# Spreading a triangular solve, turning its first result on chip, and moving two copies in a recurrence

## The chip, the cores and the metric

The kernel runs on one core of one Trainium2 chip. The metric is device time in microseconds for one execution of the whole program, the median of several runs. TensorE (PE) multiplies, VectorE (DVE) and ScalarE (ACT) work on its results, GpSimd (POOL) does part of the elementwise work, and SyncE (SP) issues most of the DMA transfers. Each engine takes its instructions strictly in the order in which the program gives them; they wait for one another by semaphores.

## The reference

Three layers follow one another: a recurrence over 768 positions for 4 x 8 heads of width 40, a mixture of experts (8 experts, two per token), and a feed-forward layer. The change concerns the recurrence alone:

```python
for t in range(S):
    y[:, :, t] = np.einsum('bhd,bhde->bhe', rt, state)
    Sa = np.einsum('bhde,bhe->bhd', state, at)
    state_decay = state * wt[:, :, None, :] - np.einsum('bhd,bhe->bhde', Sa, bt)
    state = state_decay + np.einsum('bhd,bhe->bhde', vt, kt)
```

## The kernel before

The 768 positions are cut into 24 chunks of 32. Within a chunk the effect of `a` and `b` on later positions is a triangular system of 32 x 32 for each head; its inverse, T, turns the chunk's recurrence into plain products. The 32 heads are handled in two halves, so there are 48 **steps** `g`, two for each chunk. Four chunks make a **group** of eight steps, and one **solve** makes the T of all four chunks of a group at once.

Four strands of work are woven into one order per engine:

- `chain(g)` is a step itself. `s_mm` (L602) multiplies the state by the keys, and VectorE writes the new state, `ST` (L607), scaled by `WE`. `tr` (L619) transposes the state in two pieces; ScalarE copies each out as `TRs` (L621) and `KB` (L623). `u_mm` (L589) is the next step's product with Z; ScalarE copies it into `ST` (L592). `y_mm` (L559) makes the output of the step before, and `rv_mm` (L634) a mask product that VectorE writes as `RR` (L645). One PSUM pool, `cs`, of four buffers serves five such tiles in each step, so that `u_mm` gets the buffer that `RR` of the step before was read from.
- `prepare()` scales the chunks that come two groups later. `scale` (VectorE) makes the decay `E` with a scan (L227), `R` with a second one (L231), and then `abd` (L236) and `kb` (L240). ScalarE copies parts of `E` as `WE` (L242, L243) and `Ec` (L250). `prods` (L280) makes the triangular matrices, which ScalarE writes as `Ls` and SyncE stores as `lscr`. `turns` makes four turned pieces: two of `kb`, copied as `kn` (L314) and stored as `knd`, and two of `Ec`, copied as `EN` (L325).
- `solve_group(k)` computes T of group k while group k - 1 runs. `load_l` (L437, SyncE) loads the stored matrices as `Lu`. Then VectorE does seven pairs of product and reduction (L466, L468) and after them larger products and reductions (L478, L481), two of the products on GpSimd. The result, `Tt`, is stored as `tscr` (L517).
- `apply()` loads each chunk's T from `tscr` into the diagonal blocks of `Tbd` (`tbd`, L384, four DMAs) and multiplies by it (L406), which gives `Zt` (L408). `Tbd` has two buffers, for even and odd chunks.

What stands where is set by a position that each piece of the last three strands yields, in units of groups: between the parts of a step, `fill()` lets `pump` emit all pieces whose position has been reached. A solve's pieces are spread evenly between k - 1 + s[0] and k - 1 + s[1], with the load `ll` = .06 ahead; solve 1 has its own pair, `s_1`, and solve 0 runs before the first step. `tbd` of the first chunk of a group is placed by `tl`, and L406 by `zl`.

`own_tbd()` exists for solve 0 alone: a VectorE transpose (L374) of the first chunk's part of `Tt`, and four ScalarE copies (L378) that put it into `Tbd`.

Of the kernel before, what the change touches and what calls it, by code (L numbers as in the profile page):

```python
# [24 lines left out]
PR = 8  # L25
NC = S // C
NG = NP * NC
OPT = dict(yd=(), yv=33, gix=(1, 3, 4), ye=(2, 2),  lag2=1, plan=((0, 4, -0.881), (1, 5, -0.7929), (1, 6, -0.7905), (0, 5, -0.3416), (1, 7, -0.3331), (0, 6, -0.2825), (0, 7, -0.1981), (1, 8, -0.1391)), dl=0, dk=0, ns=(0, 0), nw=(1, 1), va=1, rb=0, ra=1, kb=0, ry=(2, 2), p1=(0, 0, 0, 1, 1, 1), lw=((4, 2, 2), (6, 6, 6)), fl=((0, 1, 2, 2, 2, 2, 2, 2), (0,) * 8), lag=6, ll=.06, hurry=40, pool=(1, 4), rvpool=False, f=(3, 3, 1, 1, 1, 0), s=(.05, .72), s_1=(-.12, .62), tl=1.9, zl=.96, zd=.32, t0=-.35, nd=3, z0=8.65)
NW = 2 * PR * (C + 1)
NTB = 2  # L30
GJ = 4
# [34 lines left out]
class Rec:  # L66
# [153 lines left out]
    def scale(self, i):  # L220

        nc = self.nc
        w, a, abd, kb = self.w33[self.wx(i)], self.a[self.wx(i)], self.abd[i % 2], self.kbt(i)[0:RW]
        E = self.p2.tile([128, PR, 2, C + 1], F32, name="E")
        R = self.p2.tile([128, NW + 2], F32, name="R")
        fl = E.rearrange("p a b c -> p (a b c)")
        nc.vector.tensor_tensor_scan(out=fl[0:RW], data0=w[:, 0:NW], data1=self.d1[0:RW].rearrange("p a b -> p (a b)"),  # L227
                                     initial=0.0, op0=ALU.mult, op1=ALU.add)
        d1b = self.d1b
        nc.vector.reciprocal(out=d1b[0:RW, C + 1::C + 1], in_=fl[0:RW, C::C + 1])  # L230
        nc.vector.tensor_tensor_scan(out=R[0:RW, NW::-1], data0=w[:, ::-1], data1=d1b[0:RW, ::-1],  # L231
                                     initial=0.0, op0=ALU.mult, op1=ALU.add)
        yield
        m = lambda t: t.rearrange("p a b s c -> p (a b) s c")
        Rv = R[0:RW, 2:NW + 2].rearrange("p (a c) -> p a c", c=C + 1)[:, :, None, 0:C]
        nc.vector.tensor_tensor(out=abd[0:RW], in0=a[0:RW], in1=E[0:RW, :, :, 0:C], op=ALU.mult)  # L236
        nxt = i + 4 if i < 2 else i + 2
        if max(GJ, i + 2) <= nxt < len(self.seq) and i not in (2, 3):
            self.load_w(nxt)
        nc.vector.tensor_tensor(out=m(kb), in0=m(kb), in1=Rv.to_broadcast([RW, 2 * PR, 2, C]), op=ALU.mult)  # L240
        we = self.pwe.tile([64, 2, PR, 2], F32, name="WE")
        nc.scalar.copy(out=we[0:D, :, :, 0].rearrange("p c a -> p a c"), in_=E[0:D, :, :, C])  # L242
        nc.scalar.copy(out=we[0:D, :, :, 1].rearrange("p c a -> p a c"), in_=E[64:64 + D, :, :, C])  # L243
        self.WE[i] = we
        self.scaled[i] = E

    def decays(self, i):

        Ec = self.Ecs[i % 2]
        self.nc.scalar.copy(out=Ec[0:RW].rearrange("p a (b c) -> p a b c", b=2), in_=self.scaled.pop(i)[0:RW, :, :, 0:C])  # L250
        self.Ec[i] = Ec
# [15 lines left out]
    def prods(self, i):  # L267
# [18 lines left out]
        for out, k in ((ls, 1), (am[:, :, 64:96], 0))[:1 if i < GJ else 2]:  # L286
            nc.scalar.mul(out=out, in_=pv[:, :, k], mul=-1.0)
        (nc.scalar if i < OPT['dl'] else nc.sync).dma_start(out=self.lscr[i // GJ][i % GJ * PR:i % GJ * PR + PR].rearrange("u q t i -> (q t) u i"), in_=ls)

# [12 lines left out]
    def turns(self, i):  # L302
# [12 lines left out]
        self.KN[i] = self.pkn.tile([128, HH * D], F32, name="knd")  # L315
        (nc.scalar if i < OPT['dk'] else nc.sync).dma_start(out=self.KN[i], in_=kn.rearrange("p h d -> p (h d)"))
        if i % 2 == 0:
# [28 lines left out]
    def prepare(self):  # L346
        n = len(self.seq)
        for first, i, at in OPT["plan"]:
            yield at
            for k, _ in enumerate((self.decayed if first else self.turned)(i)):  # L350
                yield at if first or at < OPT["t0"] else at + .03 * k
        for i in range(2 * GJ, n):
            pos = iter([i / GJ - 2 + s / (6 * GJ) for s in range(6)])
            nxt = self.decayed(i + 1) if i + 1 < n else iter(())
            yield next(pos)
            next(nxt, None)
            yield next(pos)
            turned = self.turned(i)
            next(turned)
            for _ in nxt:  # L360
                pass
            for _ in range(4):
                yield next(pos)
                next(turned, None)

    def solve(self):
        for k in range(len(self.seq) // GJ):
            yield from self.solve_group(k)

    def own_tbd(self):  # L370

        nc = self.nc
        tv = self.ptm.tile([128, C * C], F32, name="tm")
        nc.vector.transpose(out=tv[0:32].rearrange("p (t x) -> p t x", x=32),  # L374
                            in_=self.Tt[0:32, 0:C * C].rearrange("p (j t) -> p t j", t=C))
        for q in range(4):
            r = slice(32 * q, 32 * q + 32)
            nc.scalar.copy(out=self.Tbd[0][r, :, r], in_=tv[0:32].rearrange("p (t u q) -> p q u t", u=PR, q=4)[:, q])  # L378

    def tbd(self, i):  # L380

# [5 lines left out]
    def apply(self):  # L387

        nc = self.nc
        for i in range(len(self.seq)):  # L390
            at = 2 * i - OPT["zl"]
            if i and i % GJ == 0:
                yield self.tau(2 * i - OPT["tl"])
                self.tbd(i)
            self.wants[2] = lambda: 2 if self.solved <= i // GJ else self.ready <= i
            z = self.Z[(i + 2) % 3]
            am, T = self.AM[i % (2 * GJ)], self.Tbd[i % NTB]
            if i < GJ:
                yield self.tau(at) if i else self.early(OPT['z0'])
                self.halves(i, am, T)  # L400
                T = self.IG
            for sg in range(2):
                yield self.tau(at + sg * OPT["zd"]) if i else self.early(OPT['z0'])
                pt = self.pp.tile([128, 512], F32, name="pp")
                for p in range(4):
                    nc.tensor.matmul(pt[0:96, p * 128:p * 128 + 128], lhsT=am[:, sg * 4 + p],  # L406
                                     rhs=T[:, sg * 4 + p, :], start=True, stop=True)
                nc.scalar.copy(out=z[0:96, sg * 4:sg * 4 + 4].rearrange("p a x -> p (a x)"), in_=pt[0:96])  # L408
            self.ZT[i] = z
            if 0 < i % GJ < GJ - 1 or i and i % GJ == 0:  # L410
                self.tbd(i + 1)
# [28 lines left out]
    def solve_group(self, k):  # L440

        nc = self.nc
# [15 lines left out]
        q, h = C // 2, C // 4  # L458
# [25 lines left out]
        for b in range(2):  # L484
            o = b * q
            p = P[:, 4 * b:4 * b + 4].rearrange("p a (c x) -> p (a c) x", x=h)
# [16 lines left out]
        pool = OPT["pool"] if k else ()  # L503
# [12 lines left out]
        self.tscr[k] = self.pd.tile([GJ * PR, 4, C, C], F32, name="tscr")  # L516
        (nc.sync if k else nc.scalar).dma_start(out=self.tscr[k].rearrange("u q j t -> (u q) (j t)"), in_=self.Tt[:, 0:C * C])  # L517
        self.solved += 1
        if k == 0:
            self.own_tbd()  # L520
            self.tbd(1)


# [1241 lines left out]
```

## Time and profile before

| | us |
|---|---|
| median of 3 runs (1272.05 to 1279.73) | 1275.37 |
| profiled execution, its own time | 1278.76 |
| its span in the profile | 1277.0 |
| recurrence within the span, about | 55 to 460 |
| experts and feed-forward layer, about | 460 to 1277 |

| engine | busy us | share |
|---|---|---|
| PE | 1148.3 | 90% |
| DVE | 857.5 | 67% |
| ACT | 724.0 | 57% |
| POOL | 533.4 | 42% |

The shares are means over three layers of different kind. From about 500 us on TensorE is busy nearly all the time. In the recurrence all engines are busy for two thirds to five sixths of the time. What ends last there is read from the stretch itself: from the waits of each engine, and from the timeline at the places where a solve ends and the next begins. In the rows "x2" means two instructions of a kind in a row; the bracket at the end of a row is the time that the engine was idle before it, and who ended that.

### The profile page before, as it was taken

Reading aid. Unit: us, or ns where it says so; the run is one execution under the profiler, and the core shown is the slowest. Engines: PE = TensorE matmul, PEld = TensorE weight load, DVE = VectorE, ACT = ScalarE, POOL = GpSimd, SP = SyncE. Lnnn points to the kernel's source line nnn. Section 1 sums busy time; section 2 is a strip of 40 time slices with the busy share of each in tenths; the row PEclk is TensorE's granted clock in tenths of the full one; section 3 lists DMA queues with packets and bytes.
Section 4 is the critical chain, followed back from the end, with each engine's and each line's share of the span. In section 5 each row is a group of like instructions: output and inputs, shape, how many; then the busy total and the mean of one; then the engine's idle time right before and its main releaser. Section 6 shows DMA issues by size and latency. Waiting matters only on the chain. (4 is left out here: it accounts for less than half of the span.)

```text
span 1277.0 us, 34710 instructions
## 1 busy us (share of the span) xinstructions
PE 1148.3 (90%) x14222; PEld 1097.6 (86%) x14222; DVE 857.5 (67%) x1610; ACT 724.0 (57%) x1517; POOL 533.4 (42%) x518
## 2 busy tenths in 40 slices
PE   6578878887877978999999999989989999999998
PEld 5477767776867868999999999989889999999998
DVE  8769697878956527558778778684466665655543
ACT  6756767766765654424434434333566666666664
POOL 6325332322635145413345344443365555543331
PEclk9688999988989977999999999989999999999999
DMA  9775867665366583645366365662541111110000
GB/s 239 195 180 135 216 159 184 170 177 153 86 120 125 105 134 120 164 141 168 94 187 192 113 190 159 207 194 75 159 112 32 31 32 34 38 34 12 12 11 21
DMA packets 143904, 156.73 MB, mean 123 GB/s; under 512 B 69867, under 2 KB 112875, under 8 KB 143723
## 3 DMA queue, kind: packets, MB, share of 16 engines
q1 hardware_dynamic: 126362, 119.86, 36.7%
q0 software_dynamic: 10752, 22.32, 6.7%
q10 hardware_dynamic: 6608, 12.06, 3.2%
q8 instruction: 122, 2.00, 0.7%
q14 instruction: 60, 0.48, 0.1%
HBM read 111.07 MB, written 43.12 MB: 121 GB/s over the span
## 5 line engine op out<-in xcount | busy, mean ns | idle before, releaser
L1637 POOL TENSOR_TENSOR gl<-fh,gh 128x1024 fp32r<-128x1024 f32 x46 | 131.1, 2878 | 105.3 <-ACT gh L1653 102.0
L1292 PE MATMUL ph<-xh,w1h 128*128 128x256 f32 (+1 forms) x576 | 159.4, 290 | 2.5 <-issue 2.5
L1292 PE MATMUL ph<-xl,w1h 128*128 128x256 f32 (+1 forms) x576 | 159.1, 289 | 0.0
L1605 PE MATMUL fps<-fxh,ih 128*128 128x256 f32 x576 | 156.4, 286 | 1.8 <-DVE fh L1607 1.8
L1605 PE MATMUL fps<-fxl,ih 128*128 128x256 f32 x576 | 153.8, 281 | 0.5 <-DVE fxl L1148 0.3
L1636 DVE TENSOR_TENSOR fh<-fh,fp 128x1024 f32<-128x1024 f32 x48 | 95.0, 2014 | 60.5 <-ACT fp L1635 60.5
L1311 PE MATMUL py<-w2h,hh 128*128 128x320 f32 x400 | 131.2, 328 | 4.3 <-ACT hh L1144 3.5
L1311 PE MATMUL py<-w2h,hl 128*128 128x320 f32 x400 | 127.0, 318 | 1.6 <-DVE hl L1146 1.6
L1311 PE MATMUL py<-w2l,hh 128*128 128x320 f32 x400 | 126.7, 317 | 2.0 <-DVE w2l L1148 1.9
L1146 DVE SCALAR_TENSOR_TENSOR hl<-ph,hh 128x512 fp32r<-128x512 f32 (+1 forms) x104 | 69.2, 665 | 82.6 <-ACT hh L1144 82.3
L1607 DVE COPY fh<-fps 128x512 f32<-128x512 f32 x96 | 64.8, 689 | 79.5 <-ACT fp L1606 74.1
L1667 PE MATMUL fpy<-oh,gl 128*128 128x320 f32 x384 | 114.6, 310 | 0.0
L1667 PE MATMUL fpy<-oh,gh 128*128 128x320 f32 x384 | 114.3, 310 | 0.0
L1667 PE MATMUL fpy<-ol,gh 128*128 128x320 f32 x384 | 113.9, 308 | 0.0
L1292 PEld LDWEIGHTS ph<-xh,w1h 128*128 128x128 f32 x576 | 111.2, 193 | 2.8 <-issue 2.7
L1292 PEld LDWEIGHTS ph<-xl,w1h 128*128 128x128 f32 x576 | 111.2, 193 | 0.3 <-DVE xl L1148 0.3
L1292 PE MATMUL ph<-xh,w1l 128*128 128x256 f32 (+1 forms) x384 | 111.0, 289 | 0.0
L1605 PEld LDWEIGHTS fps<-fxh,ih 128*128 128x128 f32 x576 | 109.0, 189 | 2.1 <-DVE fh L1607 2.0
L1605 PEld LDWEIGHTS fps<-fxl,ih 128*128 128x128 f32 x576 | 109.0, 189 | 1.1 <-DVE fxl L1148 1.1
L1605 PE MATMUL fps<-fxh,il 128*128 128x256 f32 x384 | 107.8, 281 | 0.0
L1144 ACT ACTIVATE hh<-ph 128x512 fp32r<-128x512 f32 (+1 forms) x104 | 59.9, 580 | 81.1 <-PE ph L1292 78.2
L1606 ACT ACTIVATE fp<-fps 128x512 f32<-128x512 f32 x96 | 56.1, 597 | 79.1 <-PE fps L1605 73.5
(299 smaller groups left out, 3215.5 us busy)
## 6 DMA issues: line engine op xcount, KB each, us to landing
share<-in_w_dram SPq DMA_DIRECT2D x9, 1280.0 KB
share<-in_w_dram SPq DMA_DIRECT2D x9, 1024.0 KB
wa<-in_wa_dram SPq DMA_DIRECT2D x40, 195.2 KB
knd<-kn SPq DMA_DIRECT2D x24, 320.0 KB
kb<-in_kb_dram SPq DMA_DIRECT2D x40, 192.0 KB
KB<-knd SPq DMA_DIRECT2D x24, 320.0 KB
yb<-y SPq DMA_DIRECT2D x22, 320.0 KB
ST<-in_vn_dram SPq DMA_DIRECT2D x48, 128.0 KB
```

Source lines behind the costliest of these rows:

```text
L1144: nc.scalar.activation(out=hi, in_=src, func=AF.Relu if relu else AF.Copy)
L1146: nc.vector.scalar_tensor_tensor(out=lo, in0=src, scalar=0.0, in1=hi.bitcast(F32), op0=ALU.max, op1=ALU.subtract)
L1292: nc.tensor.matmul(ph[:, m % c], lhsT=a, rhs=b, start=(q == 0), stop=(q == len(ops) - 1))
L1311: nc.tensor.matmul(py, lhsT=a[:, m, ts], rhs=b[:, m], start=(m == 0 and q == 0), stop=(m == FC - 1 and q == 2))
L1605: nc.tensor.matmul(ph[:, i], lhsT=a, rhs=b, start=(q == 0), stop=(q == len(ops) - 1))
L1606: nc.scalar.activation(out=p[:, 2 * m2:2 * m2 + 2], in_=ph, func=AF.Sigmoid, scale=-1.0)
L1607: nc.vector.tensor_copy(h[:, 2 * m2:2 * m2 + 2], ph)
L1636: mul = lambda s: nc.vector.tensor_tensor(out=h[:, s], in0=h[:, s], in1=p[:, s], op=ALU.mult)
L1637: low = lambda s: (nc.vector if last and s.start % 8 else nc.gpsimd).tensor_tensor(out=gl[:, s], in0=h[:, s], in1=gh[:, s].bitcast(F32), o ...
L1667: nc.tensor.matmul(py, lhsT=a[:, m, ts], rhs=w[:, m], start=(q == 0), stop=(q == len(ops) - 1))
```

## The change

Three things change. The solve's pieces get other positions: `s` goes from (.05, .72) to (-.06, .75), and the second value of `s_1` from .62 to .75. `own_tbd` is now called behind every solve and fills the first chunk's `Tbd`; the four loads of that chunk from `tscr` are dropped, while the three other chunks still go through `tscr`. And in the preparation of a chunk from the ninth on, the copies `WE` and `Ec` no longer follow `scale` at once, but stand behind the third turned piece of the chunk before. Since lines are added, a line of the kernel before is one to three lower in some rows of the changed one: L242, L243 and L250 become L247, L248 and L251, L287 to L325 one more, L374 becomes L377, L378 becomes L381 and L384 becomes L387.

```diff
...
-s=(.05, .72), s_1=(-.12, .62)
+s=(-.06, .75), s_1=(-.12, .75)
...
         nc.vector.tensor_tensor(out=m(kb), in0=m(kb), in1=Rv.to_broadcast([RW, 2 * PR, 2, C]), op=ALU.mult)
+        self.scaled[i] = E
+
+    def decays(self, i):
+
+        nc, E = self.nc, self.scaled[i]
         we = self.pwe.tile([64, 2, PR, 2], F32, name="WE")
         nc.scalar.copy(out=we[0:D, :, :, 0].rearrange("p c a -> p a c"), in_=E[0:D, :, :, C])
         nc.scalar.copy(out=we[0:D, :, :, 1].rearrange("p c a -> p a c"), in_=E[64:64 + D, :, :, C])
         self.WE[i] = we
-        self.scaled[i] = E
-
-    def decays(self, i):
-
         Ec = self.Ecs[i % 2]
...
-            nxt = self.decayed(i + 1) if i + 1 < n else iter(())
+            nxt = self.scale(i + 1) if i + 1 < n else iter(())
...
-            for _ in range(4):
+            for k in range(4):
                 yield next(pos)
                 next(turned, None)
+                if k == 2 and i + 1 < n:
+                    self.decays(i + 1)
...
-    def own_tbd(self):
+    def own_tbd(self, k):
...
-            nc.scalar.copy(out=self.Tbd[0][r, :, r], in_=tv[0:32].rearrange("p (t u q) -> p q u t", u=PR, q=4)[:, q])
+            nc.scalar.copy(out=self.Tbd[GJ * k % NTB][r, :, r], in_=tv[0:32].rearrange("p (t u q) -> p q u t", u=PR, q=4)[:, q])
...
-            if i and i % GJ == 0:
-                yield self.tau(2 * i - OPT["tl"])
-                self.tbd(i)
...
         self.solved += 1
+        self.own_tbd(k)
         if k == 0:
-            self.own_tbd()
             self.tbd(1)
```

ScalarE in step 13, where solve 2 ends, before. `Zt` comes from L406 of the group's last chunk, `EN` and `TRs` are the second pieces of their kind, and `ST` takes the result of `u_mm`:

```order
L408 COPY Zt_211<-pp 96x512
L325 COPY EN<-pp 64x4x2x40
L621 COPY TRs<-cs 128x256
L623 ACTIVATE KB_137<-cs 40x4x40 x2
L592 COPY ST_164<-cs 32x8x40 x2
```

and changed:

```order
L408 COPY Zt_211<-pp 96x512
L381 COPY Tbd_209<-tm 32x8x32 x4
L326 COPY EN<-pp 64x4x2x40
L621 COPY TRs<-cs 128x256
L623 ACTIVATE KB_137<-cs 40x4x40 x2
L592 COPY ST_164<-cs 32x8x40 x2
```

The four copies into `Tbd`, which read the transpose's result `tm`, stand ahead of the second pieces. On VectorE that transpose stands directly behind the last two reductions of the solve.

VectorE from `RR` of step 14 on, before:

```order
L645 TENSOR_TENSOR RR_247<-cs,mrv 64x256 x2
L607 TENSOR_TENSOR ST_164<-cs,WE 40x8x40 x2
L227 SCALAR_TENSOR_TENSOR E<-wa_140,d_155 104x528
L230 RECIPROCAL d1b<-E 104x16
L231 SCALAR_TENSOR_TENSOR R<-wa_140,d1b 104x529
L645 TENSOR_TENSOR RR_247<-cs,mrv 64x256 x2
L607 TENSOR_TENSOR ST_160<-cs,WE 40x8x40 x2
L236 TENSOR_TENSOR abd_167<-wa_140,E 104x512
L240 TENSOR_TENSOR kb_143<-kb_143,R 104x1024
L466 TENSOR_TENSOR tm<-Tt,Lu 128x4
L468 TENSOR_REDUCE Tt<-tm 128x4
```

and changed:

```order
L645 TENSOR_TENSOR RR_247<-cs,mrv 64x256 x2
L607 TENSOR_TENSOR ST_164<-cs,WE 40x8x40 x2
L466 TENSOR_TENSOR tm<-Tt,Lu 128x4
L468 TENSOR_REDUCE Tt<-tm 128x4
L466 TENSOR_TENSOR tm<-Tt,Lu 128x16
L468 TENSOR_REDUCE Tt<-tm 128x4x2
L466 TENSOR_TENSOR tm<-Tt,Lu 128x36
L468 TENSOR_REDUCE Tt<-tm 128x4x3
L466 TENSOR_TENSOR tm<-Tt,Lu 128x64
L468 TENSOR_REDUCE Tt<-tm 128x4x4
L227 SCALAR_TENSOR_TENSOR E<-wa_140,d_155 104x528
L230 RECIPROCAL d1b<-E 104x16
```

The first four pairs of solve 3 stood behind `kb` of step 15; they now stand ahead of `E`, and so ahead of `R` and of the second `RR` of the rows before, that of step 15.

SyncE between the ends of steps 13 and 15, before. `lscr` and `knd` are stores of `Ls` and `kn`, `Tbd_209` is the first chunk's buffer and `Tbd_210` the second's:

```order
L384 DMA Tbd_209<-tscr 32x8x32 x4
L288 DMA lscr<-Ls 128x8x32
L205 DMA wa_139<-in_wa_dram 48x1041 x2
L1715 DMA xd<-X 128x320
L316 DMA knd<-kn 128x640
L536 DMA ST_164<-in_vn_dram 32x1024
L541 DMA RR_243<-in_rt_dram 48x1024
L384 DMA Tbd_210<-tscr 32x8x32 x4
L205 DMA kb_141<-in_kb_dram 48x1024 x2
L257 DMA AT<-in_at_dram 64x640
L527 DMA KB_138<-knd 64x2x640
L437 DMA Lu<-lscr 128x1024
```

and changed:

```order
L289 DMA lscr<-Ls 128x8x32
L205 DMA wa_139<-in_wa_dram 48x1041 x2
L1715 DMA xd<-X 128x320
L317 DMA knd<-kn 128x640
L536 DMA ST_164<-in_vn_dram 32x1024
L541 DMA RR_243<-in_rt_dram 48x1024
L437 DMA Lu<-lscr 128x1024
L387 DMA Tbd_210<-tscr 32x8x32 x4
```

The loads of the first chunk's `Tbd` are gone, and the load of `Lu` has moved ahead of the second chunk's `Tbd`, behind the same stores and loads as before.

## Rows read from the trace of the kernel before

**Rows 1.** Windows by group: length, PE, PEld, DVE, ACT, POOL busy, clock, DMA share, GB/s.

```profile
149.00:218.50 69.50, 58.16 (x1382) 51.30 (x1380) 55.35 (x85) 48.83 (x136) 23.72 (x20) 0.95 0.71 178
218.50:288.10 69.60, 58.94 (x1382) 52.27 (x1382) 55.46 (x85) 48.89 (x136) 23.16 (x19) 0.93 0.69 174
288.10:366.80 78.70, 61.56 (x1379) 54.99 (x1379) 56.83 (x112) 48.39 (x134) 28.49 (x26) 0.85 0.51 128
```

**Rows 2.** Waits of VectorE, 120 to 460 us: in total, times, longest.

```profile
DVE RR L645 <- PE cs L634: 44.6, 12, 13.0
DVE tm L466 <- DMA Lu<-lscr: 14.4, 3, 5.5
```

**Rows 3.** Waits of TensorE in the same stretch.

```profile
PE pp L406 <- DMA Tbd<-tscr: 12.5, 4, 6.4
PE cs L589 <- ACT KB L623: 10.2, 6, 3.2
```

**Rows 4.** Timeline, end of solve 2 (start us, us, engine, line, instruction).

```profile
196.43 0.86 DVE L645 TENSOR_TENSOR RR<-cs,mrv 64x256 f32<-64x256 f32 x2
...
196.67 0.42 ACT L325 COPY EN<-pp 64x320 f32<-64x320 f32 x1
...
198.16 0.86 ACT L592 COPY ST<-cs 32x320 f32<-32x320 f32 x2 [0.29 <-PE cs L589]
198.23 2.33 DVE L481 TENSOR_REDUCE Tt<-tm 128x64 f32<-128x1024 f32 x2
...
199.59 0.81 PE L602 MATMUL cs<-ST,KB 128*40 128x40 f32 x32
...
204.25 0.77 PE L589 MATMUL cs<-ST,Zt 128*32 128x40 f32 x32 [0.52 <-DVE RR L645]
...
207.37 0.42 ACT L314 COPY kn<-pp 128x320 f32<-128x320 f32 x1
...
210.17 1.24 DVE L227 TENSOR_TENSOR_SCAN E<-wa,d 104x528 f32<-104x528 f32 x1
...
211.45 1.08 PE L406 MATMUL pp<-Tbd,share 128*96 128x128 f32 x8 [2.24 <-DMA Tbd<-tscr]
211.74 1.26 DVE L231 TENSOR_TENSOR_SCAN R<-wa,d1b 104x529 f32<-104x529 f32 x1
...
213.77 1.92 PE L406 MATMUL pp<-Tbd,share 128*96 128x128 f32 x8
...
218.49 0.86 DVE L645 TENSOR_TENSOR RR<-cs,mrv 64x256 f32<-64x256 f32 x2 [5.50 <-PE cs L634]
```

**Rows 5.** Timeline, the turn on chip behind solve 0.

```profile
41.55 5.31 POOL L264 TENSOR_TENSOR share<-AT,EN 64x320 f32<-64x320 f32 x4 [7.96 <-ACT share L287]
...
42.88 1.92 DVE L374 STREAM_TRANSPOSE tm<-Tt 32x1024 f32<-32x1024 f32 x1
...
44.84 2.59 ACT L378 COPY Tbd<-tm 32x256 f32<-32x256 f32 x4 [0.41 <-DVE tm L374]
```

**Rows 6.** Timeline: late pairs of solve 2, then start and end of solve 3.

```profile
163.02 0.43 DVE L466 TENSOR_TENSOR tm<-Tt,Lu 128x144 f32<-128x144 f32 x1
...
164.62 1.29 DVE L478 TENSOR_TENSOR tm<-Tt,Lu 128x512 f32<-128x512 f32 x2
...
220.24 0.58 SPq L437 DMA_DIRECT2D Lu<-lscr  x1
...
227.24 0.32 DVE L466 TENSOR_TENSOR tm<-Tt,Lu 128x4 f32<-128x4 f32 x1 [4.82 <-DMA Lu<-lscr]
...
230.24 0.88 DVE L645 TENSOR_TENSOR RR<-cs,mrv 64x256 f32<-64x256 f32 x2
...
265.43 0.86 DVE L645 TENSOR_TENSOR RR<-cs,mrv 64x256 f32<-64x256 f32 x2
```

**Rows 7.** Timeline: ScalarE's copies from `E` in two chunks.

```profile
169.44 0.22 ACT L242 COPY WE<-E 40x16 f32<-40x16 f32 x1 [2.88 <-DVE E L227]
...
202.65 0.62 ACT L250 COPY Ec<-E 104x512 f32<-104x512 f32 x1
```

More of the change, by code (lines that the diff above doesn't have):

```diff
@@ L27 @@
 NG = NP * NC
-OPT = dict(yd=(), yv=33, gix=(1, 3, 4), ye=(2, 2),  lag2=1, plan=((0, 4, -0.881), (1, 5, -0.7929), (1, 6, -0.7905), (0, 5, -0.3416), (1, 7, -0.3331), (0, 6, -0.2825), (0, 7, -0.1981), (1, 8, -0.1391)), dl=0, dk=0, ns=(0, 0), nw=(1, 1), va=1, rb=0, ra=1, kb=0, ry=(2, 2), p1=(0, 0, 0, 1, 1, 1), lw=((4, 2, 2), (6, 6, 6)), fl=((0, 1, 2, 2, 2, 2, 2, 2), (0,) * 8), lag=6, ll=.06, hurry=40, pool=(1, 4), rvpool=False, f=(3, 3, 1, 1, 1, 0), s=(.05, .72), s_1=(-.12, .62), tl=1.9, zl=.96, zd=.32, t0=-.35, nd=3, z0=8.65)
+OPT = dict(yd=(), yv=33, gix=(1, 3, 4), ye=(2, 2),  lag2=1, plan=((0, 4, -0.881), (1, 5, -0.7929), (1, 6, -0.7905), (0, 5, -0.3416), (1, 7, -0.3331), (0, 6, -0.2825), (0, 7, -0.1981), (1, 8, -0.1391)), dl=0, dk=0, ns=(0, 0), nw=(1, 1), va=1, rb=0, ra=1, kb=0, ry=(2, 2), p1=(0, 0, 0, 1, 1, 1), lw=((4, 2, 2), (6, 6, 6)), fl=((0, 1, 2, 2, 2, 2, 2, 2), (0,) * 8), lag=6, ll=.06, hurry=40, pool=(1, 4), rvpool=False, f=(3, 3, 1, 1, 1, 0), s=(-.06, .75), s_1=(-.12, .75), tl=1.9, zl=.96, zd=.32, t0=-.35, nd=3, z0=8.65)
 NW = 2 * PR * (C + 1)
```

## The prediction

> **What bounds the kernel now.** I read the page's stages first, then the windows by group, then the waits of the two busiest engines, and then the timeline around one group's end. The feed-forward part behind the recurrence keeps TensorE at nine tenths or more; the change touches nothing there, and it starts when the recurrence ends. So what counts is the 400 us in which the recurrence runs, one group of eight steps after the other. A group takes 69.5 to 78.7 us while chunks are prepared, and no engine fills it: in the second group VectorE is busy for 55.35 of 69.50 us, TensorE for 58.16 [rows 1]. VectorE's 14 idle us have two causes: `RR` waits for TensorE's L634, and the first product of a solve waits for the load of `Lu` [rows 2]. TensorE's longest wait is L406's for `Tbd`, 12.5 us in four places [rows 3]. Inside a solve VectorE runs without a gap and TensorE waits for it. At the end of a solve this turns over: VectorE runs out of work, TensorE waits for `Tbd`, VectorE for TensorE, and then for `Lu`. The timeline shows one such place [rows 4]: the last reductions end at 198.23 + 2.33 = 200.56, L406 starts at 211.45 after 2.24 us of waiting, and `RR` at 218.49 after 5.50. Call 196.43, where `RR` of step 12 starts, T. Then `RR` of step 15 starts at T+22.1, that of step 16 at T+33.8 and that of step 20 at T+69.0 [rows 4, 6]. I follow the same chain through the changed order.
>
> **The round trip of Tbd removed.** The four loads and L406's wait on them go: 2.24 us here, 12.5 over all solves [rows 3], which is the upper end of this gain. TensorE is also slow behind that wait: the second L406 group lasts 1.92 us, the first 1.08 [rows 4]. I count 0.9 for that and estimate 0.5 for the transposes between them in the same ratio.
>
> **The turn added.** VectorE gets one 32x1024 transpose per group. It took 1.92 us in the only row there is, with GpSimd at work beside it all that time [rows 5]. A reduction over as many elements takes 2.33/2 = 1.17 us [rows 4]. I take 1.3, nearer to that, since here the transpose follows such reductions, and keep 1.17 and 1.92 as ends. The Trainium skill (Vector Engine (DVE) Microarchitecture Reference, section 3.8) says that the transpose sustains one element per cycle per lane; with VectorE's 0.96 GHz I estimate 1024/0.96 = 1.07 us from it, which would make each group's sum below 0.2 us less. The one row here is far above that.
>
> ScalarE gets four copies, 2.59 us together [rows 5]. They stand between the copies of the two `tr` pieces of step 13 and wait for the transpose, so all that is behind them on ScalarE waits for VectorE too: `EN`, `TRs`, `KB` and the copy of `u` into `ST`, for which TensorE's L602 waits. In the kernel before, ScalarE did these from 196.67 to 198.16 + 0.86 = 199.02 [rows 4], before the reductions had ended. Now the reductions end at T+4.1, the transpose at T+5.4, the copies at T+8.0, the rest (2.35 us, as before) at T+10.4, and L602 of step 14 some 0.9 us later, at T+11.3. Before, it ended at 199.59 + 0.81 = 200.40, T+4.0. This place loses 7.3 us.
>
> From the end of that L602 to `RR` of step 15 it took 218.49 - 200.40 = 18.1 us. Off come the 2.24, the 0.9, the 0.5, and 0.5 that TensorE's `u` product waited for `RR` of step 12 [rows 4]. On comes 1.1 for `WE`, `WE` and `Ec` (0.22, 0.22 and 0.62 [rows 7]), which ScalarE now does between `EN` and `TRs` of this stretch. That leaves 15.0: TensorE is ready for `RR` 15 at T+26.3, against T+22.1. The removed loads don't pay for the stall put in their place.
>
> **The solve moved and spread.** VectorE's order shows what the new `s` does: the last reductions stay in the step in which they stood, and the first four pairs of the next solve move from behind `RR` 15 to ahead of it, and ahead of `E` and `R`. They need `Lu`. Its load moves up on SyncE, past `kb`, `AT` and `KB`, but it stays behind the store of `kn`. The second half of `kn` was copied by 207.37 + 0.42, 7.4 us behind the end of L602 of step 14 [rows 4]; now 6.9 behind T+11.3, which is T+18.2. With three issues of some 0.4 us ahead of it the load is issued at about T+19.5. From issue to the first product it took 227.24 - 220.24 = 7.0 us [rows 6]. So the solve starts at T+26.5. VectorE has nothing left to do from about T+21, so some 5 us of waiting for `Lu` stay, as long as the 4.82 of before, and now `E`, `R` and `RR` 15 stand behind it, and behind `RR` TensorE's next `u`. Five pairs took 3.0 us [rows 6], so four some 2.4; from `E` to the end of `R` is 211.74 + 1.26 - 210.17 = 2.8 [rows 4]. That puts `RR` 15 at T+31.7 instead of T+22.1.
>
> What the spread gives back comes after that. `RR`, `ST`, `abd` and `kb` of step 15 took 227.24 - 4.82 - 218.49 = 3.9; the fifth pair takes 0.6, and the sixth and seventh with the first two products 164.62 + 1.29 - 163.02 = 2.9 [rows 6]: `RR` 16 at T+39.1 against T+33.8. From there to `RR` 20 VectorE had 265.43 - 230.24 = 35.2 us without a gap; 2.9 of them now lie before it, so 32.3, and `RR` 20 starts at T+71.4 against T+69.0. **Each middle group gets 2.4 us longer.** Its bounds: 0.1 less and 0.6 more by the ends of the transpose, and some 3 us either way by when `Lu` lands.
>
> **WE and Ec moved.** ScalarE waited for `E` at several places, 2.88 us at the one shown [rows 7], and TensorE's `u` product behind such copies: 10.2 us in all [rows 3], the upper end of the gain. I take zero: that product writes a buffer of `cs` that it can have only after `RR` of the step before, and VectorE, which was late with `E`, is as late with that `RR`. The cover is VectorE's lag; where it shrinks, up to 3 us at each place are a gain. The new place costs the 1.1 us counted above.
>
> **Sum.** Solves 2 and 3: 2 x 2.4 = 4.8 us. The other three have the same terms in other sizes: one had no wait for `Tbd` to give back, one had the longest, 6.4 us [rows 3], and behind the fifth no solve follows, so no `Lu`. I take zero for these together, with 6 us either way. The profiled execution's own 1278.76 becomes 1283.6; it lies 3.4 above the median of 1275.37, so I forecast 1280. A measurement here can tell about 0.5%, 6.4 us, from no change.
>
> **Rivals.** *The bubble closes.* SyncE has four issues less, and the DMA engines, busy for 0.71 of this group [rows 1], have less to do. If `Lu` is there when VectorE comes to it, `RR` 15 starts at T+26.3 and `RR` 20 at 26.3 + 7.4 + 32.3 = T+66.0, 3 us less per group: 9 over solves 1 to 3, and some 5 more where the 6.4 us wait was. That is 14 below 1275: 1261. For it speaks that 14 idle us in each group are there to be filled; against it that the load stays behind `kn`, which the new stall makes later.
>
> *The stall costs more, and the kernel is slower.* ScalarE's part of step 13 ends at T+10.4 instead of T+2.6, so TensorE stands still for about 7 us there in each group. Behind 2.24 us of waiting it lost 1.4 in products at half speed; the mean granted clock was 0.95 in that group and 0.85 in the one with the wait of 6.4 us [rows 1, 3]. If each stall costs 2 us more in such products, `kn` and `Lu` come 2 us later at five sites: 1280 + 10 = 1290. It decides where the copies wait for VectorE longer than L406 waited for the loads; I place them at 5 us against 2.24.
>
> *The change misses the path.* If the lag of TensorE hides the copies, as it hid `EN` before, and `Lu` comes no earlier, nothing moves: 1275.
>
> **Chances.** The forecast 0.45 (its upper part already slower by the bound), the closed bubble 0.20, the costly stall 0.25, nothing moved 0.10. So faster by over 0.5% is 0.20, within it 0.44, slower 0.36. The range takes in most of both rivals: 1263 to 1294.
>
> **What would show it.** In the changed kernel's trace: L406 without a wait on `Tbd`; the first of ScalarE's `Tbd` copies in each group 4 to 6 us behind the copy before it, released by the transpose; TensorE's L634 or L602 then waiting for `TRs` or `ST`; the transpose at 1.1 to 1.9 us; VectorE still waiting for `Lu`, now with the next `RR` behind it; middle groups of 71 to 73 us. I am wrong if `Lu` is there in time, or if ScalarE doesn't wait for the transpose; then these groups fall to about 66 us.

## The result, and the profile after

The changed kernel takes 1287.42 us in the median of 11 runs (1281.9 to 1297.5), the kernel before 1275.37: a ratio of 1.0104, 95% interval 1.0075 to 1.0133, so **1% slower**. A second set of runs beside other kernels gave 1.0115 (1.0084 to 1.0146). The profiled execution took 1297.5 us, the longest of its set, with a span of 1295.7; its stages show where time went, and its total overstates the median.

First the windows by group, with the columns of [rows 1]. The bounds are other steps, the starts of `RR` in steps 4, 12, 20 and 28.

```profile
118.52:202.16 83.64, 68.22 (x1494) 60.27 (x1494) 67.83 (x93) 56.32 (x152) 29.59 (x22) 0.90 0.63 160
202.16:276.63 74.47, 61.65 (x1385) 53.43 (x1383) 58.10 (x85) 52.50 (x143) 24.57 (x18) 0.89 0.63 162
276.63:358.40 81.77, 62.92 (x1377) 55.76 (x1378) 66.56 (x117) 50.80 (x138) 22.81 (x18) 0.85 0.51 129
```

Between these steps the kernel before took 73.8, 69.0 and 77.0 us. The middle group, whose chain the prediction follows, has become 5.5 us longer; I had forecast 2.4.

The waits from 120 to 470 us, of VectorE, TensorE and ScalarE in turn (total, times, longest), against [rows 2, 3], which end at 460 us; up to 470 the kernel before waited 48.4 us for L634, and the other rows stay as they are:

```profile
DVE RR L645 <- PE cs L634: 43.4, 11, 7.9
DVE tm L466 <- DMA Lu<-lscr: 21.9, 4, 8.0
...
PE cs L634 <- ACT TRs L621: 20.2, 3, 7.0
...
PE pp L281 <- ACT EN L326: 7.6, 1, 7.6
...
ACT Tbd L381 <- DVE tm L377: 25.0, 5, 5.6
```

L406's 12.5 us of waiting for `Tbd` are gone. In their place ScalarE waits 25.0 us for the transpose, five times, and TensorE waits for what stands behind that on ScalarE: 20.2 us for `TRs` in three places and 7.6 for `EN` in a fourth. The waits for `Lu` have grown from 14.4 to 21.9 us.

The timeline at the end of solve 2 answers to [rows 4, 6]:

```profile
202.16 0.86 DVE L645 TENSOR_TENSOR RR<-cs,mrv 64x256 f32<-64x256 f32 x2
...
203.96 2.33 DVE L481 TENSOR_REDUCE Tt<-tm 128x64 f32<-128x1024 f32 x2
...
206.33 1.89 DVE L377 STREAM_TRANSPOSE tm<-Tt 32x1024 f32<-32x1024 f32 x1
...
208.26 2.56 ACT L381 COPY Tbd<-tm 32x256 f32<-32x256 f32 x4 [4.73 <-DVE tm L377]
...
211.58 1.12 PE L634 MATMUL cs<-rbd,TRs 128*64 128x64 f32 x14 [6.52 <-ACT TRs L621]
...
213.47 1.30 PE L602 MATMUL cs<-ST,KB 128*40 128x40 f32 x32
...
224.83 0.43 ACT L315 COPY kn<-pp 128x320 f32<-128x320 f32 x1 [0.80 <-PE pp L309]
225.28 0.34 SPq L317 DMA_DIRECT2D knd<-kn  x1
225.45 0.86 DVE L645 TENSOR_TENSOR RR<-cs,mrv 64x256 f32<-64x256 f32 x2 [7.92 <-PE cs L634]
...
226.70 0.36 SPq L437 DMA_DIRECT2D Lu<-lscr  x1
...
231.24 0.17 DVE L466 TENSOR_TENSOR tm<-Tt,Lu 128x4 f32<-128x4 f32 x1 [3.19 <-DMA Lu<-lscr]
```

The reader sees the chain as it was forecast: the reductions end, the transpose follows, ScalarE has stood 4.73 us for it, and TensorE gets its `TRs` 6.52 us late. Then something that the sum did not hold: L602 takes 1.30 us where the same 32 products took 0.81 [rows 4]. The windows of the stretches behind two such stalls, behind solves 2 and 3, show why, in the granted clock (the third column from the right):

```profile
211.60:224.70 13.10, 13.10 (x202) 11.16 (x202) 3.56 (x6) 7.59 (x22) 2.18 (x3) 0.50 0.48 131
286.00:290.30 4.30, 4.25 (x113) 3.60 (x113) 1.86 (x5) 2.58 (x7) 1.52 (x2) 0.59 0.29 62
```

Behind solve 2 TensorE is busy for all of 13.1 us at 0.50, the lower of its two levels (1.2 GHz), and behind solve 3 for some 3.5 us (0.59 in the mean over 4.3 us). So `kn` comes late, and `Lu` behind it.

### The profile page after: what moved, and what is told of

It is laid out like the page before. It is cut to its first block, busy times and chain, and to the rows that moved or that the text cites. A ratio compares the mean times of both kernels' runs of the same rounds, so it can differ in the third digit from the quotient of the medians.

```text
span 1295.7 us, 34714 instructions
## 1 busy us (share of the span) xinstructions
PE 1155.4 (89%) x14222; PEld 1102.6 (85%) x14222; DVE 869.2 (67%) x1615; ACT 736.5 (57%) x1537; POOL 526.9 (41%) x518
## 5 line engine op out<-in xcount | busy, mean ns | idle before, releaser
L265 POOL TENSOR_TENSOR share<-AT,EN 64x320 f32<-64x320 f32 x48 | 52.6, 1095 | 167.7 <-issue 82.0
L1607 DVE COPY fh<-fps 128x512 f32<-128x512 f32 x96 | 64.8, 689 | 79.4 <-ACT fp L1606 73.8
```

The lines of the kernel that those rows point to most:

```text
L265: self.nc.gpsimd.tensor_tensor(out=self.AM[i % (2 * GJ)][64 * ab:64 * ab + 64, :, 0:D], in0=self.AT[r, ab], in1=en[r, ab], op=ALU.mult)
L1607: nc.vector.tensor_copy(h[:, 2 * m2:2 * m2 + 2], ph)
```

## The experiments

Two theories stood against each other. **The stall**: the four copies wait for VectorE ahead of `EN` and `TRs`, and TensorE stands. **The spread**: the solve's new positions put waits for `Lu` ahead of `RR`, and the turn is free. Each part was done alone, then taken away from the whole. The table holds the times between the starts of `RR` in steps 4, 12, 20, 28 and 36 of each profile, VectorE's waits for `Lu` from 120 to 470 us, and the ratio to the kernel before.

| run | 4-12 | 12-20 | 20-28 | 28-36 | Lu | ratio (interval) |
|---|---|---|---|---|---|---|
| before | 73.8 | 69.0 | 77.0 | 56.4 | 14.4 | 1 |
| changed | 83.6 | 74.5 | 81.8 | 60.3 | 21.9 | 1.0104 (1.0075 to 1.0133) |
| e10 unchanged again | 80.9 | 75.7 | 84.1 | 60.3 | 18.8 | 1.0115 (1.0084 to 1.0146) |
| e1 turn only | 80.7 | 74.5 | 83.2 | 66.4 | 20.7 | 1.0240 (1.0215 to 1.0265) |
| e2 spread only | 80.2 | 67.9 | 75.8 | 55.5 | 36.7 | 0.9990 (0.9968 to 1.0011) |
| e3 moved copies only | 73.6 | 69.5 | 77.4 | 57.7 | 12.8 | 1.0031 (1.0011 to 1.0051) |
| e4 changed, Tbd copies late | 75.9 | 67.4 | 73.2 | 54.1 | 17.1 | 0.9925 (0.9897 to 0.9954) |
| e5 changed, Lu early | 78.5 | 69.5 | 77.9 | 59.2 | 11.7 | 1.0050 (1.0023 to 1.0077) |
| e6 changed, TensorE kept busy | 87.4 | 71.1 | 81.4 | 59.1 | 22.1 | 1.0210 (1.0172 to 1.0248) |
| e7 e4 and e5 together | 75.1 | 67.4 | 71.0 | 53.4 | 12.5 | 0.9897 (0.9862 to 0.9931) |
| e8 e4, WE and Ec as before | 80.2 | 67.8 | 76.5 | 55.0 | 21.3 | 0.9950 (0.9919 to 0.9982) |
| e9 e6, in the stalls alone | 82.8 | 72.4 | 80.0 | 58.7 | 23.8 | 1.0070 (1.0044 to 1.0095) |
| e11 spread only, Lu early | 79.0 | 65.9 | 76.5 | 56.8 | 28.7 | 0.9937 (0.9907 to 0.9967) |
| e12 late turn only | 75.5 | 73.4 | 80.2 | 58.8 | 21.2 | 1.0079 (1.0055 to 1.0103) |

The mean granted clock from `RR` of step 4 to that of step 45 was 0.92 before, 0.89 and 0.88 in the two profiles of the changed kernel, 0.88 in e1, 0.94 in e4 and e7, and 0.95 in e9.

### e1: the turn alone

```diff
-    def own_tbd(self):
+    def own_tbd(self, k):
...
-            if i and i % GJ == 0:
-                yield self.tau(2 * i - OPT["tl"])
-                self.tbd(i)
...
         self.solved += 1
+        self.own_tbd(k)
         if k == 0:
-            self.own_tbd()
```

> The kernel before, with the turn of each group's first T on chip as the only change; positions of the solve and the copies of WE and Ec stay as they were. Theory (the stall): ScalarE waits 4 to 6 us for the transpose, TensorE then stands for 6 to 7 us and runs at half clock behind it, so RR of step 15 comes some 9 us later than before; of that the wait for Lu that follows (4.8) is given back. Middle groups 73 to 74 us against 69, ratio to the kernel before 1.010 to 1.016, some 1290 us. Rival (the spread costs the time, the turn is free): ratio 0.995 to 1.002, and no wait of ScalarE for the transpose above 2 us.

Measured 1.024, 1306.28 us: slower than the whole change. The waits of ScalarE, TensorE and VectorE:

```profile
ACT Tbd L378 <- DVE tm L374: 24.5, 5, 6.1
...
PE cs L631 <- ACT TRs L618: 24.7, 5, 6.7
...
DVE tm L463 <- DMA Lu<-lscr: 20.7, 4, 6.5
```

The turn alone brings the whole stall, and with it more than the whole loss; how much of this is the stall's is read from e12, where the turn stands without it. The expectation's sum missed twice: `RR` of step 15 came 5.1 us later than before and not 9, and nothing was given back at `Lu`, which was waited for about as long as before (4.4 us behind solve 2, against 4.8). The two misses offset each other, so that the group came out at 74.5, close to the 73 to 74 expected. The other groups lost 6 to 10 us each, and the ratio is above the expected band.

### e2: the spread alone

```diff
-s=(.05, .72), s_1=(-.12, .62)
+s=(-.06, .75), s_1=(-.12, .75)
```

> The kernel before, with the solve's new positions as the only change: four pairs of the next solve ahead of RR of step 15, the load of Lu ahead of the second chunk's Tbd; L406 still waits for the loads of Tbd. Theory (the spread is sound, the stall eats it): kn is not late here, so Lu is there at T+17 to T+19, RR of step 15 at T+22 to T+24, and the work now done in the bubble comes off behind it: middle groups 63 to 65 us, ratio 0.980 to 0.990, some 1257 us. Rival (the spread moves the wait for Lu ahead of RR and gains nothing, or costs): ratio 0.998 to 1.006, waits for Lu above 10 us in all.

Measured 0.999: no change. My theory of a gain of 1 to 2% fell; the rival was right for the total, not for each group. The timeline of the gap between solves 2 and 3, SyncE's issues with `kn` and the first product:

```profile
210.40 2.54 SPq L384 DMA_DIRECT2D Tbd<-tscr  x4
...
212.45 0.42 ACT L314 COPY kn<-pp 128x320 f32<-128x320 f32 x1
...
215.47 0.37 SPq L316 DMA_DIRECT2D knd<-kn  x1
...
217.41 0.37 SPq L437 DMA_DIRECT2D Lu<-lscr  x1
...
223.16 0.17 DVE L466 TENSOR_TENSOR tm<-Tt,Lu 128x4 f32<-128x4 f32 x1 [7.84 <-DMA Lu<-lscr]
```

`kn` is there at 212.87, but its store waits 2.6 us more in SyncE's queue, behind the four `Tbd` loads (2.54 us) and what follows them. Then `Lu` takes 5.75 us. The spread gains 1.1 us in this group, and loses 6.4 in the one before it, where the longest wait for `Lu` is 11.6 us.

### e3: the moved copies of WE and Ec alone

```diff
-            nxt = self.decayed(i + 1) if i + 1 < n else iter(())
+            nxt = self.scale(i + 1) if i + 1 < n else iter(())
...
+                if k == 2 and i + 1 < n:
+                    self.decays(i + 1)
```

> The kernel before, with ScalarE's copies of WE and Ec behind the third turned piece as the only change. Theory (VectorE's lag covers them): ratio 0.998 to 1.002, ScalarE's 10 us of waiting for E gone and VectorE's waits as long as before. Rival (the cover is thin): TensorE's 10 us of waiting for ScalarE behind these copies come off, ratio 0.990 to 0.995.

Measured 1.0031: a little over the expected band, with an interval clear of no change, so a small loss. ScalarE's 9.8 us of waiting for `E` are gone, as expected. TensorE's waits for `KB` fell from 10.2 to 2.2 us, but nothing was gained by it: `RR`, which waited 48.4 us for L634 from 120 to 470 us, waits 57.9, where no change was expected.

### e4: the copies into Tbd behind the transpose, not waiting for it

```diff
+        if k:
+            yield k - 1 + .83
         for q in range(4):
             r = slice(32 * q, 32 * q + 32)
...
-        self.solved += 1
-        self.own_tbd(k)
+        yield from self.own_tbd(k)
+        self.solved += 1
```

> The changed kernel, with the transpose where it is and ScalarE's four copies into Tbd some 0.08 of a group later, between the two tr pieces of step 14, when the transpose is long done. No work is left out. Theory (the stall is the whole loss, and the half clock hangs on it): ScalarE's waits for the transpose fall from 25 us to under 2, TensorE's for TRs behind them go, the granted clock behind the end of a solve stays above 0.8, the middle groups fall from 74.5 to 62 to 66 us, ratio to the kernel before 0.980 to 0.988. Rival (the transpose's 1.9 us on VectorE and the four pairs ahead of RR carry the loss): the middle groups stay above 71 us, ratio above 1.003.

Measured 0.9925, 1264.53 us: faster than both kernels, a little short of the expected band; the middle group takes 67.4 us against 74.5, where 62 to 66 were expected. The timeline at the end of solve 2 (`RR` of step 12 at 192.58):

```profile
196.75 1.96 DVE L378 STREAM_TRANSPOSE tm<-Tt 32x1024 f32<-32x1024 f32 x1
...
199.17 2.57 ACT L384 COPY Tbd<-tm 32x256 f32<-32x256 f32 x4
...
208.55 0.37 SPq L440 DMA_DIRECT2D Lu<-lscr  x1
...
212.92 0.17 DVE L469 TENSOR_TENSOR tm<-Tt,Lu 128x4 f32<-128x4 f32 x1 [2.97 <-DMA Lu<-lscr]
```

The copies start without a wait. From 120 to 470 us ScalarE waits for the transpose once, 0.4 us, and TensorE's products never for `TRs` or `Tbd`. The same work in another place turns 1% slower into 0.75% faster. So the stall, together with the half clock behind it, costs the changed kernel 1.8%.

### e8: the same, with WE and Ec copied where they were

```diff
-            nxt = self.scale(i + 1) if i + 1 < n else iter(())
+            nxt = self.decayed(i + 1) if i + 1 < n else iter(())
...
-                if k == 2 and i + 1 < n:
-                    self.decays(i + 1)
```

> The changed kernel with the four copies into Tbd 0.08 of a group later, and WE and Ec copied where they were before, directly behind the scaling. Theory (the moved copies of WE and Ec cost 1.1 us of ScalarE ahead of TRs in each group and give nothing, as they did alone at 1.003): ratio 0.988 to 0.991. Rival (where VectorE's lag is shorter, TensorE's waits for ScalarE behind these copies count, and the move pays): ratio 0.994 to 1.000.

Measured 0.995. It lies on the rival's side, but its interval and that of e4 overlap, and the two ran at different times: whether the move pays in this company stays open.

### e5 and e7: Lu ahead of the store of kn

```diff
-ll=.06
+ll=.14
```

> The changed kernel, with the load of Lu some 0.08 of a group earlier: ahead of the store of kn, right behind the store of lscr. Theory (Lu is late because it stands behind kn, and the stall makes kn late): VectorE's waits for Lu, 21.9 us in all, fall below 6; RR of step 15 then hangs on TensorE's L634 alone, at about T+31.5 instead of T+34.5; middle groups some 71.5 us against 74.5; ratio to the kernel before 0.997 to 1.003 against 1.010. ScalarE's 25 us of waiting for the transpose stay. Rival (the load is slow or blocks SyncE, wherever it stands): waits for Lu above 15 us, ratio 1.007 to 1.014.

Measured 1.005, between the two bands. The stall is still there (18.4 us of waiting for the transpose), the waits for `Lu` fall to 11.7, not below 6, and the middle group to 69.5, further than the 71.5 expected; `RR` of step 15 comes at T+27.9, not T+31.5. So `Lu` behind a late `kn` is a part of the loss, at most the half that went. Some of the group's 5.0 us may be the clock's: in this profile it was back 4.4 us behind the stall, not 13.

> The changed kernel with both: the four copies into Tbd 0.08 of a group later, and the load of Lu ahead of the store of kn. Theory: with the stall gone only the waits for Lu are left at a solve's start, 17 us in all; they fall below 6, RR of step 15 moves from T+26 to T+23, middle groups from 67 to 64 us, ratio to the kernel before 0.980 to 0.987. Rival (L634 ends as late as Lu lands): the waits move to RR, ratio 0.990 to 0.995, like the late copies alone.

Measured 0.9897, 1265.16 us against 1277.9 for the kernel before beside it: the fastest ratio, but the gain over e4 is within the intervals. The rival was right. Behind solve 2 the wait for `Lu` falls from 2.97 us to 0.45, but `RR` of step 15 now waits 1.47 us for L634, and the group stays at 67.4. In total (VectorE, 120 to 470 us; L634 is L637 here; in e4 29.6 for it, 5.7 for a transposing product and 17.1 for `Lu`):

```profile
DVE RR L648 <- PE cs L637: 31.9, 9, 8.5
DVE tm L469 <- DMA Lu<-lscr: 12.5, 4, 5.2
```

### e11: the spread alone, with Lu early

The edits of e2 and of e5 on the kernel before.

> The kernel before with the solve's new positions and the load of Lu 0.08 of a group earlier, ahead of the store of kn; the first chunk's Tbd still loaded. Theory (the spread alone gave nothing because Lu was still behind kn and the Tbd loads): waits for Lu fall from 36.7 to below 22 us, ratio to the kernel before 0.986 to 0.994. Rival (L406's wait for Tbd then takes its place as the bound): ratio 0.997 to 1.003.

Measured 0.9937: the ratio expected, with less off the waits for `Lu` than expected (28.7 us, and L406 still waits 10.2 for `Tbd`). The middle group takes 65.9 us, the shortest of all, without any turn. So the spread pays where `Lu` is loaded ahead of `kn`: alone it reaches about what it reaches with the late turn (0.9925, e4).

### e12: the late turn alone

The edits of e1, with the four copies late as in e4.

> The kernel before with the turn of each group's first T on chip, its four copies 0.08 of a group behind the transpose; the solve's positions and the copies of WE and Ec as before. Theory (the turn pays where ScalarE doesn't wait for it): TensorE's 12.5 us of waiting for Tbd go, VectorE's 1.9 us per solve come; ratio to the kernel before 0.993 to 0.999. Rival (the transpose stands on VectorE's path and no bubble is left to pay for it without the spread): ratio 1.002 to 1.008.

Measured 1.0079: the rival. L406 no longer waits and ScalarE only 0.7 us, yet the middle group grows by 4.4 us.

```profile
204.81 1.96 DVE L375 STREAM_TRANSPOSE tm<-Tt 32x1024 f32<-32x1024 f32 x1
...
209.70 2.57 ACT L381 COPY Tbd<-tm 32x256 f32<-32x256 f32 x4
```

The transpose (1.96 us) stands ahead of `E` and of `RR` 13 on VectorE, and the copies (2.57 us) ahead of `kn` and `TRs` on ScalarE, against 2.24 us saved at L406; and `Lu` is still waited for. The clock may have a part in it too: its mean was 0.86 in this group, 0.93 in the same one before. The turn alone does not pay in either of the two places tried for its copies, and with the stall gone a third of e1's loss stays (1.008 of 1.024).

Nor do the runs show that the late turn pays beside the spread. The pair that differs by it alone, e8 and e2, stands at 0.9950 and 0.9990, with intervals that overlap; so do those of e7 and e11 (0.9897 and 0.9937), which differ by the moved copies as well.

### e6 and e9: TensorE kept busy through the stall

```diff
+        if self.busy:
+            fill = rv[0].rearrange("p q x -> p (q x)")
+            for x in range(0, 2 * FILL):
+                nc.tensor.matmul(fill[:, x % 2 * 128:x % 2 * 128 + 128], lhsT=self.ident, rhs=self.ident, start=True, stop=True)
+            self.busy = False
         for p in range(4):
             for sg in range(2):
```

> The changed kernel, with TensorE kept busy in the stall: ahead of the L634 that follows each turn on chip it multiplies a constant 128 x 128 matrix by itself 30 times, into the buffer that L634 then writes. Nothing is left out; the work is added. Theory (the clock that falls behind the stall is what the forecast of 1280 missed): the granted clock behind the end of solve 2, 0.50 to 0.52 over 17 us, stays above 0.9; kn's second copy comes 3 us sooner behind the end of L602, the middle group takes some 71.5 us against 74.5, ratio 1.001 to 1.006. Rival (the clock lies off the path): the clock rises, the group stays above 74, ratio 1.009 to 1.015. Third: the clock falls all the same.

Measured 1.021: slower, against the expectation, and for a plain reason. Behind solves 1 and 5 TensorE's stall lies at another instruction, ahead of L634, so that there the added 7.2 and 8.5 us came on top: `RR` of step 37 stood 19.8 us behind that of step 36, and 11.8 in the changed kernel. Behind solve 2, where the work lies in the stall, the group took 71.1 us, as expected. e9 puts the work into the stalls of solves 1 to 4 alone:

> The changed kernel with the same 30 multiplications of a constant matrix, now only where TensorE stands anyway: behind solves 2, 3 and 4 ahead of L634, as in the run before, behind solve 1 ahead of the second tr piece, and none behind solve 5. Nothing is left out. Theory (the fallen clock behind the stall is part of the loss): no wait of TensorE's gets longer, the clock in the 20 us behind each of these stalls stays above 0.9, middle groups 71 to 72 us, and the time is 0.3 to 0.7% below the unchanged kernel of this call. Rival (the clock lies off the path): within 0.2% of it.

> The changed kernel as it stands, once more beside the others, for a second profile. Theory: ratio to the kernel before 1.008 to 1.013; the stall of 6.5 to 7.5 us stands in every profile, the length of the half clock behind it differs from site to site (13 us behind solve 2, 4 us behind solve 3 in the first profile). Rival: the first profile was odd, the clock stays up, ratio below 1.007.

e10 came out about as its theory said: 1.0115, with stalls of 6.4 to 7.0 us ahead of L634. The clock was low for 13 us behind solve 2 again, but behind solve 3 for 12 us, where the first profile had 3.5. e9 measured 1.007 beside it, 1285.23 against 1292.75 us: 0.45% by the ratios and 0.58% by the medians, though the two intervals still touch. The windows of the 13 us behind the stall of solve 2, e9 and then the unchanged kernel:

```profile
212.10:225.20 13.10, 12.94 (x288) 11.46 (x287) 5.37 (x10) 9.32 (x27) 2.46 (x3) 1.00 0.74 198
```

```profile
209.70:222.70 13.00, 12.91 (x204) 11.06 (x204) 3.56 (x6) 7.68 (x23) 2.29 (x3) 0.51 0.51 132
```

At full clock TensorE gets 288 matmul instructions done in the time in which it got 204 done, and `RR` of step 14 comes at T+18.4 instead of T+23.0. With work added and nothing taken away, the group takes 72.4 us (71 to 72 expected), 3.3 shorter than in e10 and 2.0 shorter than in the first profile. The stretch from L602 (L604 in e9) to the second half of `kn` shows the same, 213.25 + 0.81 to 220.39 + 0.42, which is 6.75 us against 10.5:

```profile
213.25 0.81 PE L604 MATMUL cs<-ST,KB 128*40 128x40 f32 x32
...
220.39 0.42 ACT L316 COPY kn<-pp 128x320 f32<-128x320 f32 x1
```

So behind solve 2 the clock is a part of the loss; for the whole time it is likely, not certain, as the intervals touch. 1.007 remains with the clock up.

## Why the prediction came out as it did

The range held the time, and the direction was right. That says little by itself: the range was 31 us wide and held two of the three rivals, and a loss of over 0.5%, as measured, had a chance of 0.36. The likeliest value, 1280, was 7 us low. By its steps:

- **The round trip removed**: right. L406 waits for `Tbd` nowhere.
- **The turn**: the place and the order of the waits were right: 4.73 us for the transpose (I said 4 to 6), 6.52 us of TensorE's standing (about 7). The transpose was mis-sized: 1.89 us where I took 1.3, though the one row I had said 1.92 [rows 5]. I put that row's length down to GpSimd beside it; here GpSimd stood idle from 201.05 to 211.34. The four copies took 2.56.
- **From the stall to kn: the step that failed.** I gave it 6.9 us from L602's end to the second half of `kn`, the 7.4 of [rows 4] less the 0.5 of a wait that goes, and so priced it at full clock; it took 225.26 - 214.77 = 10.5, with L602 itself 0.5 longer. In e9, where the clock stayed up, the same stretch took 220.81 - 214.06 = 6.75 us. So the length was right for full clock, and the half clock, which I had only as a rival at 2 us a site, cost 3.7 here. In e6, with the clock up as well, `kn` ended at T+18.5 (forecast T+18.2), `RR` 15 came at T+30.0 (T+31.7) and the group took 71.1 us (71.4).
- **The solve moved**: `Lu` was issued at T+24.5 (I said T+19.5, all of it `kn`'s lateness) and took 4.5 us, not 7.0. The wait for it was 3.2 instead of 5; `E`, `R` and `RR` 15 stood behind it as forecast, and `RR` 15 came at T+34.5 (T+31.7). That it was not 5 us late, like the issue, is luck: the faster landing gave 2.5 of them back.
- **What the spread gives back**: right to 0.2 us. From `RR` 15 to `RR` 16 7.6 us (7.4), from there to `RR` 20 32.3 (32.3).
- **WE and Ec at zero**: close; 1.003 alone.
- **The other three sites at zero**: mis-sized, at the upper end of my 6 us either way. In the profile, from its start to `RR` 12 the change costs 5.7 us, from 28 to 36 3.9, and from there to `RR` 45 it gives 3.6 back: 6.0. Solves 2 and 3 cost 5.5 and 4.8 where I had 2.4 each, and in e10 6.7 and 7.1. Together `RR` 45 comes 16.3 us later, 474.40 against 458.15; the medians differ by 12.

So what happened is the costly stall (1290), of which the forecast was the milder form. The closed bubble was wrong for this kernel. Its time, 1261 or 0.989, came out in a neighbour, e7 at 0.9897, but its condition did so only in part: behind solve 2 the wait for `Lu` was down to 0.45 us there, over all solves it was still 12.5.

One more reading failed, outside the prediction. In the expectation of e2 I took `Lu` to follow `kn` by a few issues. SyncE's queue was itself late: 2.5 of the 2.6 us by which the store of `kn` waited there are the four loads that the turn removes. The parts of this change are not additive: 1.024, 0.999 and 1.003 alone make 1.010 together.

## What to carry to other kernels

When a round trip through memory is replaced by work on the engines, look at what stands behind the new instruction in the order of the engine that will wait for it: four copies that waited 5 us for VectorE held up TensorE for 6.5, and the same copies 0.08 of a group later held up nobody (e4). Price a stall of TensorE with the products that follow it at half clock as well, here 3.7 us behind one stall of 6.5; a stretch behind an existing long wait in the trace shows them. And try the parts of a change alone before adding up their effects, since a part that frees a queue can be what makes another one work.

## What the runs showed of the hardware

The 32x1024 transpose takes 1.88 to 1.91 us in all six places of the changed kernel's profile, with GpSimd at work or idle, and up to 2.02 us in the other runs (e8): 1.6 times as long as a reduction over as many elements, or a little more. The Trainium skill (Vector Engine (DVE) Microarchitecture Reference, section 3.8) gives one element per cycle per lane, from which I had estimated 1.07 us; no run here shows that rate for this form, whose input is read with a stride.

Behind stalls of like length (6.4 to 7.0 us) the clock stayed at its lower level for 13 us in two profiles behind solve 2, and for 4.4 us there in e5; behind solve 3 it did so for 3.5 us in the first profile of the changed kernel and for 12 in the second (e10):

```profile
285.50:297.50 12.00, 11.97 (x197) 10.34 (x198) 3.56 (x6) 7.15 (x21) 2.22 (x3) 0.50 0.53 143
```

In all of them TensorE was busy from the stall on. So the same place of the same program has either length, and one profile does not give the price of a stall. What decides between them is open. From its issue to the first product, `Lu` took 4.2 us (e7) to 7.1 (e12) behind solve 2; what sets that was not tried.
